# One full 128-column weight load ahead of each set of four 32-column matmuls, in an attention backward pass

## The chip, the cores and the metric

The kernel runs on one core of a Trainium2 chip. The metric is the device time in microseconds (us) of one execution. The kernel before takes 732.7 us (median of 6 runs, 732.21 to 733.62). "Span" is the time from the first to the last instruction of the one execution that was profiled. It is about 1.8 us shorter than the time that was measured of it.

Names: PE is the matrix engine, PEld its weight loads, DVE, ACT and POOL the vector, scalar and general engines, SPq the queue that issues the large transfers. PEclk is the clock granted to PE, as a share of full speed, as the profile shows it.

## The reference, cut to what matters

One token passes a layer of attention over a cache of 8192 positions, with 32 heads of 128, and an MLP beside it. The reference returns the layer's output and the gradients of all inputs and weights.

```python
scores = einsum("bhqd,bhkd->bhqk", q, k) * Dh ** -0.5     # 32 heads, 8192 positions, Dh = 128
p      = softmax(scores)
o      = einsum("bhqk,bhkd->bhqd", p, v)
out    = x + o.reshape(...) @ wo + mlp(xn)
# and by jax.vjp: d_x, d_k_cache, d_v_cache, d_wq, d_wo, d_w1, d_w3, d_w2
```

With a single query, the gradients of K and V are outer products as large as the caches. So 2.10 MB of K and 2.10 MB of V are read for each head, and as many bytes are written: the kernel moves 303.58 MB and does little arithmetic on them.

## The kernel before

K and V of a head lie in tiles of 2.10 MB, of which there are ten. A tile is loaded, turned by PE in 512-column steps, used for the products, **overwritten in place** by its gradient, stored, and only then free for the next load.

```python
def T(h, kind, c):                     # four 128x128 f32 transposes, then one ACT copy
    ...
    for k in range(4):
        nc.tensor.transpose(pT[:, k * P:(k + 1) * P], W3[:, 4 * c + k, :], ident_f[:])
    ...

def Mp(h, kind, c0):                   # "score product": 4 matmuls, one per column tile of 32
    ...
    for c in (c0, c0 + 1):
        ...
        for par in range(2):
            q = QW * (2 * (c - c0) + par)
            o = QL + QW * (2 * a + par) - c0
            nc.tensor.matmul(S_[kind][q:q + QW, :], lhsT=S_["qz"][:, o:o + QW], rhs=KTb[:, par, :],
                             start=(c0 == 0), stop=(c0 == NCH - 2), skip_group_check=True)

def wsum(h, kind, a):                  # "sum product": 16 matmuls, four rounds over the column tiles
    ...
    for i in range(NI):
        q = QW * (i % 4)
        o = QW - 4 + QW * i - 4 * slot
        nc.tensor.matmul(xg["X"][q:q + QW, :], lhsT=Z[:, o:o + QW], rhs=W[:, N4 * i:N4 * (i + 1)], ...)
    ...

def store(kind, h):                    # both in the one queue of SPq, in this order
    ...
    fifo((dkc if kind == "K" else dvc)[h], t[:])
    free_slots.append(t)
    load_next()                        # the next K or V, into the tile that became free longest ago

def outers_a(h):                       # DVE, on the head before
    outer_v(h, 0, J // 2)
    outer_v(h, J // 2, J)
    store("V", h)
    outer_k(h, 0, J // 2)
```

Each head has eight score products and two sum products. The MLP runs once, ahead of head 2.

## Time and profile before

| | kernel before |
|---|---|
| median time, span of the profiled run | 732.7 us, 730.6 us |
| bytes moved, mean rate | 303.58 MB, 416 GB/s |
| rate from 290 to 668 us | 428 GB/s |
| matmuls and weight loads on PE | 5669 and 5669 |
| V gradient of head 2 stored, first transposes of K of head 31, output copy | 122.14, 674.60, 718.11 us |

The prediction shows the slices and the time of a head. What bears on the change besides is the cost of the narrow matmuls and their loads. In the table of groups, "busy, mean ns of one" comes after the first bar; after the second comes the idle time of the engine just before these instructions, and what ended most of it.

```profile
L417 PE MATMUL X<-kv,Z 128*32 128x512 bf16 x1024 | 85.3, 462 | 1.8 <-DVE Z L434 1.8
...
L324 PEld LDWEIGHTS <-qz 128*32 128x32 bf16 x1024 | 26.6, 93 | 42.8 <-issue 41.6
L417 PEld LDWEIGHTS <-Z 128*32 128x32 bf16 x1024 | 28.6, 110 | 33.9 <-issue 16.6
```

1024 sum matmuls take 85.3 us of PE, 83 ns each, although the record gives 462 ns for one: they run side by side. The four of a score product show it best: together they take 0.41 us, and one of them 0.40 us (median of L324). "Issue" is idle time of the load path in which it waited for nothing that the profile shows. Much of it stands ahead of the score products (L324), where PE goes over from 128-wide to 32-wide work.

### The profile page before, as it was taken

Reading aid. Unit: us, or ns where it says so; the run is one execution under the profiler, and the core shown is the slowest. Engines: PE = TensorE matmul, PEld = TensorE weight load, DVE = VectorE, ACT = ScalarE, POOL = GpSimd, SP = SyncE. Lnnn points to the kernel's source line nnn. Section 1 sums busy time; section 2 is a strip of 40 time slices with the busy share of each in tenths; the row PEclk is TensorE's granted clock in tenths of the full one; section 3 lists DMA queues with packets and bytes.
Section 4 is the critical chain, followed back from the end, with each engine's and each line's share of the span. In section 5 each row is a group of like instructions: output and inputs, shape, how many; then the busy total and the mean of one; then the engine's idle time right before and its main releaser. Section 6 shows DMA issues by size and latency. Waiting matters only on the chain.

```text
span 730.6 us, 13869 instructions
## 1 busy us (share of the span) xinstructions
PE 606.6 (83%) x5669; PEld 423.1 (58%) x5669; DVE 459.3 (63%) x806; ACT 369.4 (51%) x719; POOL 29.9 (4%) x45
## 2 busy tenths in 40 slices
PE   3989589998899889988987887888898889978940
PEld 2657466666566656666655555566566556655620
DVE  4069646677757776776646765547756756667482
ACT  2650736656556556554655554545554536655510
POOL 0010110000100000001000000000000000000000
PEclk9996699999999999988998998979897969989765
DMA  9999999999999999999999999999999999999993
GB/s 354 400 411 420 425 421 432 415 429 425 417 416 426 429 427 421 430 428 426 425 428 426 431 423 427 429 428 428 427 424 429 429 427 428 428 434 426 425 393 155
DMA packets 27145, 303.58 MB, mean 416 GB/s; under 512 B 2807, under 2 KB 4153, under 8 KB 10441
## 3 DMA queue, kind: packets, MB, share of 16 engines
q1 hardware_dynamic: 21328, 276.39, 89.5%
q0 software_dynamic: 5728, 26.30, 8.9%
q8 instruction: 44, 0.72, 0.4%
q14 instruction: 21, 0.16, 0.1%
q10 hardware_dynamic: 24, 0.01, 0.0%
HBM read 151.34 MB, written 151.34 MB: 414 GB/s over the span
## 4 chain that ended last, share of the span: by engine, by line
PE 42%; DMA 41%; DVE 8%; ACT 6%; issue 1%; SPq 0%; ACTq 0%; DVEq 0%
DMA out_dram<-kv 22%; PE pT L305 20%; DMA kv<-in_A_k_cache_dram 11%; DMA kv<-in_A_v_cache_dram 7%; PE m L340 6%; PE X L417 5%; ACT KT L307 4%; PE sA L324 4%; DVE kv L450 3%; PE dA L324 2%; DMA wo_g<-in_A_wo_dram 2%; DVE side L251 1%; PE gu_ps L527 1%; ACT KT L330 1%; PE m L430 1%
## 5 line engine op out<-in xcount | busy, mean ns | idle before, releaser
L307 ACT COPY KT<-pT 128x512 f32<-128x512 f32 x512 | 289.5, 589 | 235.3 <-PE pT L305 200.6
L305 PE MATMUL pT<-ident_f,kv 128*128 128x128 f32 x2048 | 318.7, 296 | 40.6 <-DMA kv<-in_A_k_cache_dram 17.9
L305 PEld LDWEIGHTS pT<-ident_f,kv 128*128 128x128 f32 x2048 | 248.5, 154 | 97.0 <-PE pT L305 27.8
L450 DVE TENSOR_TENSOR kv<-qd,U 128x4096 bf16<-128x4096 bf16 x64 | 146.0, 2284 | 0.0
L450 DVE TENSOR_TENSOR kv<-qd,P 128x4096 bf16<-128x4096 bf16 x64 | 143.6, 2284 | 0.0
L340 PEld LDWEIGHTS m<-selc,KT 128*128 128x128 f32 x512 | 67.4, 205 | 45.8 <-ACT KT L330 34.1
L340 PE MATMUL m<-selc,KT 128*128 128x16 f32 x512 | 73.2, 276 | 22.7 <-ACT KT L330 22.5
L417 PE MATMUL X<-kv,Z 128*32 128x512 bf16 x1024 | 85.3, 462 | 1.8 <-DVE Z L434 1.8
L400 DVE SCALAR_TENSOR_TENSOR U<-m,P 128x64 bf16<-128x64 f32 x32 | 7.4, 233 | 104.9 <-PE m L340 104.9
L324 PE MATMUL dA<-KT,qz 128*32 128x512 bf16 x512 | 55.2, 418 | 0.2 <-ACT KT L307 0.2
L324 PE MATMUL sA<-KT,qz 128*32 128x512 bf16 x512 | 55.1, 421 | 0.0
L324 PEld LDWEIGHTS <-qz 128*32 128x32 bf16 x1024 | 26.6, 93 | 42.8 <-issue 41.6
L417 PEld LDWEIGHTS <-Z 128*32 128x32 bf16 x1024 | 28.6, 110 | 33.9 <-issue 16.6
L366 DVE TENSOR_REDUCE mrow<-m 128x1 f32<-128x64 f32 x32 | 7.1, 223 | 62.9 <-PE m L340 62.9
L360 ACT CAST qd<-pT 128x256 bf16<-128x256 f32 x32 | 11.9, 372 | 48.6 <-DVE kv L450 32.4
L500 DVE SCALAR_TENSOR_TENSOR wq_g<-wq_g,side 128x512 bf16<-128x512 bf16 x40 | 27.3, 683 | 0.0
L251 DVE SCALAR_TENSOR_TENSOR side<-wo_g,g_bc 128x640 bf16<-128x640 bf16 x32 | 26.2, 819 | 1.1 <-DMA wo_g<-in_A_wo_dram 0.8
L373 DVE TENSOR_REDUCE negM<-m 128x1 f32<-128x128 f32 x32 | 9.3, 291 | 24.5 <-PE m L370 24.5
L432 DVE SCALAR_TENSOR_TENSOR U<-m,P 128x128 bf16<-128x128 f32 x32 | 11.4, 355 | 18.0 <-PE m L430 18.0
L390 DVE RECIPROCAL rZ<-m 128x1 f32<-128x1 f32 x32 | 5.3, 167 | 24.1 <-PE m L384 24.1
L330 ACT COPY KT<-dA 128x512 f32<-128x512 f32 x32 | 19.3, 604 | 0.6 <-PE dA L324 0.6
L330 ACT COPY KT<-sA 128x512 f32<-128x512 f32 x32 | 19.3, 603 | 0.0
(154 smaller groups left out, 365.2 us busy)
## 6 DMA issues: line engine op xcount, KB each, us to landing
out_dram<-kv SPq DMA_DIRECT2D x64, 2048.0 KB, 31.1
kv<-in_A_k_cache_dram SPq DMA_DIRECT2D x32, 2048.0 KB, 25.2
kv<-in_A_v_cache_dram SPq DMA_DIRECT2D x32, 2048.0 KB, 26.3
out_dram<-wo_g POOLq DMA_DIRECT2D x8, 640.0 KB, 11.4
out_dram<-wq_g POOLq DMA_DIRECT2D x8, 640.0 KB, 12.9
wq_g<-in_A_wq_dram POOLq DMA_DIRECT2D x7, 640.0 KB, 13.2
wo_g<-in_A_wo_dram POOLq DMA_DIRECT2D x7, 640.0 KB, 19.3
kv<-in_B_w_dram SPq DMA_DIRECT2D x2, 1728.0 KB, 28.7
```

The lines of the kernel that those rows point to most:

```text
L251: nc.vector.scalar_tensor_tensor(junk[:], G_["wo"][:, hh, :], 1.0, g_bc[:], ALU.mult, ALU.mult, accum_out=G_["do"][:, hh:hh + 1])
L305: nc.tensor.transpose(pT[:, k * P:(k + 1) * P], W3[:, 4 * c + k, :], ident_f[:])
L307: nc.scalar.copy(KT[:].rearrange("p k w -> p (k w)"), pT[:])
L324: nc.tensor.matmul(S_[kind][q:q + QW, :], lhsT=S_["qz"][:, o:o + QW], rhs=KTb[:, par, :], start=(c0 == 0), stop=(c0 == NCH - 2), skip_grou ...
L330: nc.scalar.copy(XS[:].rearrange("p k w -> p (k w)"), S_.pop(kind)[:])
L340: nc.tensor.matmul(S_["m"][:, b0:b0 + J].rearrange("p (c k t) -> p k c t", k=4, t=2)[:, k, :, :], lhsT=XS[:, k, :], rhs=selc[:].rearrange( ...
L360: nc.scalar.copy(qd[:].rearrange("p a d -> p (a d)"), hd[h].pop("ps_r"))
L373: nc.vector.tensor_reduce(S_["negM"][:], S_["m"][:, 2 * J:2 * J + P], AX.X, ALU.max, negate=True)
L417: nc.tensor.matmul(xg["X"][q:q + QW, :], lhsT=Z[:, o:o + QW], rhs=W[:, N4 * i:N4 * (i + 1)], start=(slot == 0 and i < 4), stop=(slot == NS ...
L432: nc.vector.scalar_tensor_tensor(S_["U2"][:], S_["V"][:, 0:J].unsqueeze(2).to_broadcast([P, J, 2]), S_["m"][:, OC + NS:OC + NS + 1], S_["P ...
L450: nc.vector.tensor_tensor(dst[:, lo * DH:hi * DH].rearrange("p (j a b) -> p j a b", a=DH // 2, b=2), vec.rearrange("p (a b) -> p a b", b=2 ...
L500: nc.vector.scalar_tensor_tensor(wq_g[:, ci, :], wq_g[:, ci, :], 1.0, dqb, ALU.mult, ALU.mult, accum_out=dxa[:, ci, g:g + 1])
```

## The change

Four narrow loads were to become one full one: the four 32-column weights are laid beside each other, one 128-column load is meant to bring in all four, and the four matmuls are marked as holding their weights. The query tile becomes wider for this (and is filled by two small copies), and the vectors of the MLP move into the unused end of a weight tile, to make room.

```diff
-        qz = consts.tile([P, QL + 4 * QW], BF16, name=f"qz{i}")
+        qz = consts.tile([P, QL + 8 * QW], BF16, name=f"qz{i}")
...
+    def held_matmul(out, lhsT, rhs, q, start, stop):
+        E = nc.tensor
+        E.add_instruction(mybir.InstMatmult(
+            ... tile_size=(P, QW), tile_position=(0, q), ..., ldweights=False, ...))
... in Mp
+        o = QL + 2 * QW * 2 * a - c0
+        nc.tensor.ldweights(S_["qz"][:, o:o + P])
-                nc.tensor.matmul(S_[kind][q:q + QW, :], lhsT=S_["qz"][:, o:o + QW], rhs=KTb[:, par, :], ...)
+                held_matmul(S_[kind][q:q + QW, :], S_["qz"][:, o + q:o + q + QW], KTb[:, par, :], q, ...)
... in wsum
-            nc.tensor.matmul(xg["X"][q:q + QW, :], lhsT=Z[:, o:o + QW], rhs=W[:, N4 * i:N4 * (i + 1)], ...)
+            if i % 4 == 0:
+                nc.tensor.ldweights(Z[:, o:o + P])
+            held_matmul(xg["X"][q:q + QW, :], Z[:, o:o + QW], W[:, N4 * i:N4 * (i + 1)], q, ...)
... in mlp, and likewise for eight more vectors
-        sig = consts.tile([P, NB], F32, name="sig")
+        sig = mt(NB)
```

More of the change, by code (lines that the diff above doesn't have):

```diff
@@ L308, in T @@
         hd[h]["kt"][(kind, c)] = KT
+    def held_matmul(out, lhsT, rhs, q, start, stop):
+        E = nc.tensor
+        E.add_instruction(mybir.InstMatmult(
+            name=nc.get_next_instruction_name(), engine=mybir.EngineType.PE,
+            start_tensor_calc=start, stop_tensor_calc=stop, tile_size=(P, QW), tile_position=(0, q),
+            bass_skip_group_check=True, ldweights=False,
+            ins=[E.lower_ap(rhs), E.lower_ap(lhsT, for_matmul_weights=True)], outs=[E.lower_ap(out)]))
     def Mp(h, kind, c0):
@@ L322, in Mp @@
                 q = QW * (2 * (c - c0) + par)
-                o = QL + QW * (2 * a + par) - c0
-                nc.tensor.matmul(S_[kind][q:q + QW, :], lhsT=S_["qz"][:, o:o + QW], rhs=KTb[:, par, :],
-                                 start=(c0 == 0), stop=(c0 == NCH - 2), skip_group_check=True)
+                held_matmul(S_[kind][q:q + QW, :], S_["qz"][:, o + q:o + q + QW], KTb[:, par, :], q,
+                            c0 == 0, c0 == NCH - 2)
     def ev(h, kind):
@@ L346, in fill_qz @@
         g, hh = divmod(h, GH)
-        nc.vector.tensor_copy(
-            hd[h]["qz"][:, QL:QL + 4 * QW].rearrange("p (a t n) -> p a t n", t=2, n=QW)[:, :, :, 0:2],
-            grp[g]["cm"][:, :, :, hh, :].rearrange("p t a m -> p a t m"))
+        for r in range(2):
+            nc.vector.tensor_copy(
+                hd[h]["qz"][:, QL:QL + 8 * QW].rearrange("p (a r t n) -> p r a t n", r=2, t=2, n=QW)[:, r, :, :, 0:2],
+                grp[g]["cm"][:, :, :, hh, :].rearrange("p t a m -> p a t m"))
     def rows_pe(h, ps, first):
@@ L416, in wsum @@
             o = QW - 4 + QW * i - 4 * slot
-            nc.tensor.matmul(xg["X"][q:q + QW, :], lhsT=Z[:, o:o + QW], rhs=W[:, N4 * i:N4 * (i + 1)],
-                             start=(slot == 0 and i < 4), stop=(slot == NS - 1 and i >= NI - 4),
-                             skip_group_check=True)
+            if i % 4 == 0:
+                nc.tensor.ldweights(Z[:, o:o + P])
+            held_matmul(xg["X"][q:q + QW, :], Z[:, o:o + QW], W[:, N4 * i:N4 * (i + 1)], q,
+                        slot == 0 and i < 4, slot == NS - 1 and i >= NI - 4)
         if slot == NS - 1:
@@ L519, with mt @@
     blocks_f = [(b, min(P, F - b * P)) for b in range(NB)]
-    hcol = consts.tile([P, NB], F32, name="hcol")
+    mt_f = mA[:, NA * F:].bitcast(F32)
+    mt_at = [0]
+    def mt(cols):
+        r = mt_f[:, mt_at[0]:mt_at[0] + cols]
+        mt_at[0] += cols
+        return r
+    hcol = mt(NB)
     def mlp():
@@ L546, in mlp @@
                                  start=False, stop=True, skip_group_check=True)
-        gu = consts.tile([P, 2, NB], F32, name="gu")
-        nc.vector.memset(gu[:], 0.0)
+        gu = mt(2 * NB).rearrange("p (w b) -> p w b", w=2)
+        nc.vector.memset(gu, 0.0)
         nc.vector.tensor_copy(gu[:, :, 0:NFULL], gu_ps[:, :, 0:NFULL])
@@ L553, in mlp @@
         up = gu[:, 1, :]
-        dhc = consts.tile([P, NB], F32, name="dhc")
-        nc.vector.tensor_reduce(dhc[:], dh_ps[:], AX.X, ALU.add)
-        sig = consts.tile([P, NB], F32, name="sig")
-        nc.scalar.activation(sig[:], gate, ACTF.Tanh, scale=0.5)
-        nc.vector.tensor_scalar(sig[:], sig[:], 0.5, 0.5, ALU.mult, ALU.add)
-        silu = consts.tile([P, NB], F32, name="silu")
-        nc.vector.tensor_tensor(silu[:], gate, sig[:], ALU.mult)
-        nc.vector.tensor_tensor(hcol[:], silu[:], up, ALU.mult)
@@ L562, in mlp @@
-        hcol_bf = consts.tile([P, NB], BF16, name="hcol_bf")
-        nc.vector.tensor_copy(hcol_bf[:], hcol[:])
-        dgu = consts.tile([P, 2, NB], F32, name="dgu")
-        nc.vector.tensor_tensor(dgu[:, 1, :], dhc[:], silu[:], ALU.mult)
-        t1 = consts.tile([P, NB], F32, name="t1")
-        nc.vector.tensor_scalar(t1[:], sig[:], -1.0, 1.0, ALU.mult, ALU.add)
-        nc.vector.tensor_tensor(t1[:], t1[:], gate, ALU.mult)
-        nc.vector.tensor_scalar(t1[:], t1[:], 1.0, None, ALU.add)
@@ L570, in mlp @@
-        nc.vector.tensor_tensor(t1[:], t1[:], sig[:], ALU.mult)
-        nc.vector.tensor_tensor(dgu[:, 0, :], dhc[:], up, ALU.mult)
-        nc.vector.tensor_tensor(dgu[:, 0, :], dgu[:, 0, :], t1[:], ALU.mult)
-        dgu_bf = consts.tile([P, 2, NB], BF16, name="dgu_bf")
-        nc.vector.tensor_copy(dgu_bf[:], dgu[:])
+        dhc = mt(NB)
+        nc.vector.tensor_reduce(dhc, dh_ps[:], AX.X, ALU.add)
+        sig = mt(NB)
+        nc.scalar.activation(sig, gate, ACTF.Tanh, scale=0.5)
+        nc.vector.tensor_scalar(sig, sig, 0.5, 0.5, ALU.mult, ALU.add)
@@ new lines, in mlp @@
+        silu = mt(NB)
+        nc.vector.tensor_tensor(silu, gate, sig, ALU.mult)
+        nc.vector.tensor_tensor(hcol, silu, up, ALU.mult)
+        hcol_bf = mt(NB // 2).bitcast(BF16)
+        nc.vector.tensor_copy(hcol_bf, hcol)
+        dgu = mt(2 * NB).rearrange("p (w b) -> p w b", w=2)
+        nc.vector.tensor_tensor(dgu[:, 1, :], dhc, silu, ALU.mult)
+        t1 = mt(NB)
+        nc.vector.tensor_scalar(t1, sig, -1.0, 1.0, ALU.mult, ALU.add)
+        nc.vector.tensor_tensor(t1, t1, gate, ALU.mult)
@@ L575, in mlp @@
+        nc.vector.tensor_scalar(t1, t1, 1.0, None, ALU.add)
+        nc.vector.tensor_tensor(t1, t1, sig, ALU.mult)
+        nc.vector.tensor_tensor(dgu[:, 0, :], dhc, up, ALU.mult)
+        nc.vector.tensor_tensor(dgu[:, 0, :], dgu[:, 0, :], t1, ALU.mult)
+        dgu_bf = mt(NB).bitcast(BF16).rearrange("p (w b) -> p w b", w=2)
+        nc.vector.tensor_copy(dgu_bf, dgu)
         for b, rows in blocks_f:
```

## The prediction

> **What bounds the kernel now.** I read the page first, from its slices (part 2): 40 slices of 18.3 us.
>
> ```profile
> PE 606.6 (83%) x5669; PEld 423.1 (58%) x5669; DVE 459.3 (63%) x806; ACT 369.4 (51%) x719; POOL 29.9 (4%) x45
> ...
> DMA  9999999999999999999999999999999999999993
> GB/s 354 400 411 420 425 421 432 415 429 425 417 416 426 429 427 421 430 428 426 425 428 426 431 423 427 429 428 428 427 424 429 429 427 428 428 434 426 425 393 155
> DMA packets 27145, 303.58 MB, mean 416 GB/s; under 512 B 2807, under 2 KB 4153, under 8 KB 10441
> ```
>
> The DMA row is 9 in every slice but the last, at 425 to 430 GB/s. The bytes alone need 303.58 MB / 428 GB/s = 709 us of the 730.6 us span. PE at 83% looks close, so I then asked how long one head takes. The row maximum (L366) runs once per head, and its starts in the timeline give the period. Where no DMA wait stands in the way, four heads go from 162.48 to 235.17 us, 18.2 us a head (the bare head is 17.4 us; each fourth carries group work). From 290.13 to 668.37 us, 18 heads take 21.0 us each. A head moves 4 x 2.10 MB of K and V and their gradients, and a quarter of a group's 4 x 0.655 MB of wq and wo: 9.04 MB, at 428 GB/s 21.1 us. So in the steady part a head waits for bytes, and compute has 21.1 - 18.2 = **2.9 us of slack per head**. The windows view says the same: PE is busy 329 of 378 us, at a granted clock of 0.88[...], against 1.00 in an unhindered head.
>
> ```profile
> core 0: us, PE busy (x) PEld busy (x) DVE busy (x) ACT busy (x) POOL busy (x), PEclk, DMA share, GB/s
> 290.00:668.00 378.00, 328.81 (x2963) 226.81 (x2962) 238.31 (x393) 197.82 (x395) 12.19 (x15) 0.88 1.01 428
> ...
> 233.87:251.24 17.37, 15.52 (x152) 10.81 (x152) 13.63 (x24) 10.40 (x22) 0.00 (x0) 1.00 1.01 427
> ```
>
> Only the **tail** is set by compute: the last heads' work after the last loads landed. In the timeline, K of head 31 (issued at 649.72 us) lets the transposes go at 674.57; the profile names the ACT copy that ended at 674.47, but the PE queue's own semaphore event for a load also stands at 674.5, and such a load takes 25.2 us (median), so I put this wait down to the DMA. From there to the output copy at 718.11 every step is compute, and the last tiny stores end the span at 730.6.
>
> [...] each score product, 32 columns wide, comes after 128-wide transposes with a gap called "issue" of 0.17 us (L324: 41.6 us in all, 223 times), and the next transposes wait about 0.24 us again. [...] 20 full bf16 loads at L488 take 0.74 us together, 37 ns apart, and four 32-column ones at L324 take 0.10 us. So a full load is no cheaper than two narrow ones, and not free. [...]
>
> **The change part by part.** The intent is one full load in place of four narrow ones. The order of the built program says otherwise: the matmuls marked as holding their weights still have **a narrow load each in front of them**. Score and sum products have 2048 matmuls and 2048 narrow loads before and after (L324 and L417 become L312), and 512 full loads are added (L327 and L428, 256 each). Nothing is removed on PE; PE weight loads should go from 5669 to 6181. And each full load[...] stands between 32-wide work.
>
> 1. Score products (8 a head, 4 matmuls each). The full load follows transposes or selection matmuls, also 128-wide[...]. It adds its own time, 0.04 to 0.1 us: 8 x 0.05 = 0.4 us a head.
>
> 2. Sum products (2 a head, 16 matmuls each) are the costly part.
>
> ```profile
> 576.12 0.10 PEld L324 LDWEIGHTS <-qz 128*32 128x32 bf16 x4 [0.17 <-issue]
> 576.12 0.41 PE L324 MATMUL sA<-KT,qz 128*32 128x512 bf16 x4
> ...
> 576.37 0.55 PEld L417 LDWEIGHTS <-Z 128*32 128x32 bf16 x16
> 576.37 1.05 PE L417 MATMUL X<-kv,Z 128*32 128x512 bf16 x16
> ...
> 577.35 0.86 PEld L305 LDWEIGHTS pT<-ident_f,kv 128*128 128x128 f32 x8 [0.42 <-PE X L417]
> ```
>
> Sixteen matmuls pass from 576.37 to 577.35, 0.98 us[...]. The cost of an isolated group of four is read from a score product: its loads begin at 578.37, and the next transposes' loads begin at 578.71, 0.34 us. With a full load of 0.05 to 0.1 us between groups a group becomes about 0.40 us, four 1.6 us[...]: +0.7 us per sum product at full clock. At half clock (granted from about 675 to 686 us) groups are 0.43 us apart now; an isolated score product takes 0.55 us there (645.80 to 646.35), with its load about 0.7: +1.2 us[...].
>
> 3. DVE: 32 more small copies into the query tile, 32 x 0.167 = 5.3 us of 730, in gaps (DVE is 63% busy), off the path. The MLP vectors only change address, into the unused end of a weight tile; the next K or V load into it waits for the gradient store of that weight anyway. Bytes are unchanged.
>
> Sum per head at full clock: 0.4 + 2 x 0.7 = 1.8 us, of which the first sum product partly falls in a PE wait that exists (2 us before L340 at 260.17, for an ACT copy). 18.2 + 1.8 = 20.0 us, still below 21.1. So the steady part **stays with the DMA and costs nothing**. In the tail after 674.57 the path holds the two sum products of head 30 at half clock (2 x 1.2), the first one of head 31 (0.7, the second lies behind 9 us of outer products on DVE), and some 6 score products (6 x 0.05 = 0.3): 3.4 us. 732.3 + 3.4 = 735.7; I say **735.5 us**.
>
> **The rivals.** (a) *All hidden*: the full loads are pulled ahead[...], or delays vanish in the wait for V of head 31. For it: the PE queue runs loads early elsewhere. Against it: [...] V of head 31 leaves at most 2.3 us (its semaphore event at 686.6, its transposes at 688.95). Then 732 to 733. (b) *PE becomes the bound*: if a mode switch costs twice my figure, a head gets 3.6 us more, 21.8 us, over the 21.1 of the DMA, and some 28 heads after the MLP lose 0.7 us each: with the longer tail, 750 us or more. For it: the gap from sum products to transposes is 0.42 us, more than I took for a group's end. Against it: most of that gap is the streaming of the last matmuls, which I counted. The buffer of ten tiles also smooths the heads. (c) *Faster*, as intended: if the chip skipped a narrow load whose weights are there. Nothing in the built program asks for that, and even a free PE could only shorten the tail by some 2 us, since 709 us of bytes and a start at the first loads remain.
>
> **Range and chances.** Low end 731.8: rival (a), with run-to-run noise (732.21 to 732.84). High end 741: the tail at twice its estimate, 7 us, or half clock lasting longer[...], and 1 to 2 us. Leaving the 2% band downward needs 717.7 us, which no PE change reaches here; upward it needs 747, which takes rival (b). I give 0.01 faster, 0.94 same, 0.05 slower.
>
> **What would show each step.** PE weight loads 6181 and 512 full ones: right on the build. Sum products' time from first load to the next transposes near 1.7 us instead of 0.98, with "issue" gaps before L312[...]. DMA row and GB/s unchanged through slice 38, and heads between 290 and 668 us still 21.0 us apart: the slack held. The output copy about 3 us later than 718.11, and the transposes of K of head 31 still near 674.6: the tail. If instead L366 comes every 21.5 us or more and the waits for K and V landings at L305 (17.9 and 12.9 us) are gone, PE has become the bound and I was wrong about the switch; if the sum products still pass in 1.0 us, the full loads hid.

Where "mode" or "switch" stands, read the change between 128 and 32 columns; what the trace of the kernel before shows of it is the gap of 0.17 us at L324. That loads run early is measured: the last four loads of the sum product at 576.37 us are through at 576.93, and its last four matmuls run from 577.03 to 577.42.

Without it a sum product costs 4 x 0.40 - 0.98 = 0.62 us at full clock, where the text has 0.7, and 4 x 0.7 - 4 x 0.43 = 1.08 us at half clock, where it has 1.2. A head then comes to 0.4 + 2 x 0.62 = 1.6 us (the text: 1.8), the tail to 2 x 1.08 + 0.62 + 0.3 = 3.1 us (3.4), and the time to 732.3 + 3.1 = 735.4 us. Compared with the result below are 3.4 and 735.5. All of these costs are estimates from the times beside them.

## The result, and the profile after

The changed kernel takes **736.8 us** (median of 6 runs, 735.79 to 738.06) where the kernel before takes 732.7. The ratio is 1.0058, with a 95% interval from 1.0045 to 1.0071: slower by 4.2 us of 732.7, within the 2% band. Here and below a ratio is the mean time of one kernel's fast runs over that of the other's of the same rounds, so it isn't quite the ratio of the medians. All outputs are right. The run profiled was one of the slower ones, 737.98 us with a span of 736.2 us, 5.6 us over that of before.

From the page of the changed kernel, the counts and the slices of 18.4 us (the line of GB/s reads from left to right; slice 7 is 110 to 129 us):

```profile
PE 639.5 (87%) x5669; PEld 459.9 (62%) x6181; DVE 462.6 (63%) x838; ACT 367.8 (50%) x719; POOL 30.0 (4%) x45
...
DMA  9999998999999999999999999999999999999993
GB/s 347 401 408 422 430 429 355 398 422 412 424 424 425 427 426 427 424 427 428 424 425 426 428 428 420 431 427 428 424 424 427 432 425 432 429 425 433 418 393 143
```

PE weight loads go from 5669 to 6181 and matmuls stay at 5669: nothing was removed, 512 full loads were added. And the transfers have a hole that they did not have before: 355 and 398 GB/s in slices 7 and 8, where the prediction's page of the kernel before has 432 and 415.

The added loads in the table of groups:

```profile
L312 PE MATMUL X<-kv,Z 128*32 128x512 bf16 x1024 | 114.2, 436 | 12.0 <-DVE Z L445 2.0
...
L428 PEld LDWEIGHTS <-Z 128*128 128x128 bf16 x256 | 25.0, 98 | 72.1 <-issue 63.2
...
L327 PEld LDWEIGHTS <-qz 128*128 128x128 bf16 x256 | 28.9, 113 | 0.2 <-issue 0.2
```

Both groups load the same 128 columns, 256 times. Those of the score products (L327) have no idle time ahead of them. Those of the sum products (L428) have 72.1 us, 63.2 of it "issue". The timeline shows one sum product of the changed kernel (start and duration in us first):

```profile
667.23 0.10 PEld L428 LDWEIGHTS <-Z 128*128 128x128 bf16 x1 [0.24 <-DVE Z L445]
667.34 0.10 PEld L312 LDWEIGHTS <-Z 128*32 128x32 bf16 x4
...
667.66 0.10 PEld L428 LDWEIGHTS <-Z 128*128 128x128 bf16 x1 [0.23 <-issue]
667.77 0.10 PEld L312 LDWEIGHTS <-Z 128*32 128x32 bf16 x4
668.10 0.10 PEld L428 LDWEIGHTS <-Z 128*128 128x128 bf16 x1 [0.23 <-issue]
668.21 0.10 PEld L312 LDWEIGHTS <-Z 128*32 128x32 bf16 x4
668.54 0.10 PEld L428 LDWEIGHTS <-Z 128*128 128x128 bf16 x1 [0.23 <-issue]
668.64 0.10 PEld L312 LDWEIGHTS <-Z 128*32 128x32 bf16 x4
668.98 0.75 PEld L305 LDWEIGHTS pT<-ident_f,kv 128*128 128x128 f32 x7 [0.23 <-issue]
```

Ahead of each of its four 128-wide loads, and of the transposes' loads at the end, the load path stands idle for 0.23 to 0.24 us; but for the first, the profile names nothing that was waited for ("issue"). From the first load to the next transposes 1.75 us pass, where the prediction reads 0.98 us in the kernel before: **+0.77 us per sum product, twice a head**. A score product is different:

```profile
672.52 0.10 PEld L327 LDWEIGHTS <-qz 128*128 128x128 bf16 x1
672.72 0.10 PEld L312 LDWEIGHTS <-qz 128*32 128x32 bf16 x4
...
673.06 0.31 PEld L305 LDWEIGHTS pT<-ident_f,kv 128*128 128x128 f32 x3 [0.24 <-PE pT L305]
```

From its narrow loads to the next transposes 0.34 us pass, as in the kernel before:

```profile
578.37 0.10 PEld L324 LDWEIGHTS <-qz 128*32 128x32 bf16 x4 [0.17 <-issue]
...
578.71 0.53 PEld L305 LDWEIGHTS pT<-ident_f,kv 128*128 128x128 f32 x5 [0.24 <-PE pT L305]
```

The full load follows 128-wide transposes without a gap, and the narrow loads start 0.10 us after its end; before, they stood behind a gap of 0.17 us anyway. The added load fits into the gap that was there.

Now where the 5.6 us came in. The first heads, in the windows view (the last three columns are PEclk, the DMA engines' share and GB/s), first of the kernel before, then of the changed one:

```profile
core 0: us, PE busy (x) PEld busy (x) DVE busy (x) ACT busy (x) POOL busy (x), PEclk, DMA share, GB/s
120.00:124.00 4.00, 4.00 (x38) 2.94 (x34) 4.00 (x2) 3.37 (x8) 0.00 (x0) 1.00 1.00 420
124.00:128.00 4.00, 3.70 (x31) 2.72 (x32) 3.14 (x10) 2.89 (x7) 0.00 (x0) 1.00 1.03 440
...
132.00:140.00 8.00, 7.15 (x74) 5.20 (x70) 5.42 (x7) 4.52 (x10) 0.00 (x0) 1.00 1.01 416
```

```profile
120.00:124.00 4.00, 3.86 (x38) 2.77 (x43) 1.95 (x5) 1.17 (x2) 0.00 (x0) 1.00 0.93 392
124.00:128.00 4.00, 3.96 (x37) 2.86 (x41) 4.00 (x3) 2.15 (x4) 0.00 (x0) 1.00 0.21 84
...
132.00:140.00 8.00, 7.33 (x84) 5.17 (x90) 5.08 (x13) 4.47 (x11) 0.00 (x0) 1.00 0.94 360
```

The changed kernel's transfers stop almost wholly for 4 us, at 84 GB/s, because nothing was left to move: the next thing in the queue was a gradient that had not been computed (SPq waits 13.3 us for DVE's product there). The store of V of head 2, from the timeline of SPq, before and after:

```profile
122.14 0.34 SPq L105 DMA_DIRECT2D out_dram<-kv  x1
```

```profile
127.26 0.34 SPq L105 DMA_DIRECT2D out_dram<-kv  x1
```

It comes 5.1 us later. The row maximum, once a head, says where the compute fell behind; the two kernels' lines for heads 2 and 3:

```profile
109.24 0.22 DVE L366 TENSOR_REDUCE mrow<-m 128x1 f32<-128x64 f32 x1 [9.56 <-PE m L340]
124.98 0.22 DVE L366 TENSOR_REDUCE mrow<-m 128x1 f32<-128x64 f32 x1
```

```profile
113.60 0.22 DVE L376 TENSOR_REDUCE mrow<-m 128x1 f32<-128x64 f32 x1 [9.68 <-PE m L349]
130.92 0.22 DVE L376 TENSOR_REDUCE mrow<-m 128x1 f32<-128x64 f32 x1 [0.74 <-PE m L349]
```

Head 3 follows head 2 after 15.7 us before and 17.3 us after: 1.6 us more, two sum products at 0.77. Head 2 itself stands 4.4 us late: 2.1 us had been lost by the row maximum of head 1 (44.91 to 47.03 us; 0.7 of it by that of head 0, which no sum product precedes), and the rest between head 1 and head 2, where the sum products of head 1 and the MLP lie. That stretch varies by some 2 us between executions all the same: it is 62.96 us in e2 and 64.63 in e3 (below), neither with full loads there, and 64.33 before.

An account of bytes puts the loss in its places. The transfers run at some 428 GB/s when they have work. The MB that a stretch of the trace falls short of that rate, from the rates of its 10 us windows, divided by 428 GB/s, is time lost (the end is that of the span):

| MB short of 428 GB/s | 0 to 120 us | 120 to 150 | 150 to 650 | 650 to 680 | 680 to end | all |
|---|---|---|---|---|---|---|
| before | 2.50 | 0.17 | 0.85 | -0.08 | 5.70 | 9.14 |
| after | 2.36 | **1.99** | 1.21 | -0.04 | 5.99 | 11.51 |
| difference, us | -0.3 | **+4.3** | +0.8 | +0.1 | +0.7 | +5.5 |

The hole at 120 to 150 us costs 4.3 of 5.5 us. It is never made good: in no later column is the changed kernel less short than the kernel before. That is why the transposes of K of head 31 start at 680.25 us, not 674.60, and the output copy comes at 723.14, not 718.11. From the one to the other it is 42.9 us after and 43.5 us before. That does not make the full loads free there: from 674 to 686 us the granted clock was 0.57 before and 0.86 after. What they cost at the end is read from e7 below.

### The profile page after: what moved, and what is told of

Read it like the earlier page. It is cut to its first block, busy times and chain, and to the rows that moved or that the text cites. A ratio compares the mean times of both kernels' runs of the same rounds, so it can differ in the third digit from the quotient of the medians.

```text
span 736.2 us, 14414 instructions
## 1 busy us (share of the span) xinstructions
PE 639.5 (87%) x5669; PEld 459.9 (62%) x6181; DVE 462.6 (63%) x838; ACT 367.8 (50%) x719; POOL 30.0 (4%) x45
## 4 chain that ended last, share of the span: by engine, by line
PE 59%; DMA 13%; ACT 9%; DVE 7%; PEld 5%; issue 5%; SPq 0%; ACTq 0%; DVEq 0%
PE pT L305 26%; PE X L312 10%; PE m L349 8%; DMA kv<-in_A_k_cache_dram 7%; PE sA L312 6%; ACT KT L307 6%; DMA out_dram<-kv 5%; PE dA L312 2%; PEld pT L305 2%; DVE kv L461 2%; DVE side L251 2%; DMA wo_g<-in_A_wo_dram 1%; ACT kv L619 1%; ACT KT L339 1%; PE gu_ps L546 1%
## 5 line engine op out<-in xcount | busy, mean ns | idle before, releaser
L305 PE MATMUL pT<-ident_f,kv 128*128 128x128 f32 x2048 | 314.3, 293 | 16.0 <-DMA kv<-in_A_k_cache_dram 12.5
L305 PEld LDWEIGHTS pT<-ident_f,kv 128*128 128x128 f32 x2048 | 244.6, 153 | 64.1 <-PE pT L305 30.3
L312 PE MATMUL X<-kv,Z 128*32 128x512 bf16 x1024 | 114.2, 436 | 12.0 <-DVE Z L445 2.0
L349 PE MATMUL m<-selc,KT 128*128 128x16 f32 x512 | 70.0, 269 | 11.3 <-ACT KT L339 11.3
L349 PEld LDWEIGHTS m<-selc,KT 128*128 128x128 f32 x512 | 63.7, 195 | 25.0 <-ACT KT L339 18.4
L428 PEld LDWEIGHTS <-Z 128*128 128x128 bf16 x256 | 25.0, 98 | 72.1 <-issue 63.2
L327 PEld LDWEIGHTS <-qz 128*128 128x128 bf16 x256 | 28.9, 113 | 0.2 <-issue 0.2
L312 PEld LDWEIGHTS <-Z 128*32 128x32 bf16 x1024 | 26.7, 95 | 3.0
```

Source lines behind the costliest of these rows:

```text
L312: E.add_instruction(mybir.InstMatmult(name=nc.get_next_instruction_name(), engine=mybir.EngineType.PE, start_tensor_calc=start, stop_tenso ...
L327: nc.tensor.ldweights(S_["qz"][:, o:o + P])
L349: nc.tensor.matmul(S_["m"][:, b0:b0 + J].rearrange("p (c k t) -> p k c t", k=4, t=2)[:, k, :, :], lhsT=XS[:, k, :], rhs=selc[:].rearrange( ...
L428: nc.tensor.ldweights(Z[:, o:o + P])
```

## The experiments

Twelve kernels ran, each in five rounds beside the kernel before. "MB short" is the column 120 to 150 us of the account above, from the one profiled run.

| run | what it is | median us | ratio to before, 95% interval | MB short, 120 to 150 |
|---|---|---|---|---|
| e1_first3 | full loads in heads 0 to 2 only | 737.48 | 1.0056 [1.0038, 1.0074] | 1.80 |
| e2_from3 | full loads in heads 3 to 31 only | 735.51 | 1.0033 [1.0018, 1.0048] | 0.12 |
| e3_noload | no full loads, all else of the change | 734.10 | 1.0011 [0.9996, 1.0027] | 0.72 |
| e4_narrow | the added loads made 32 columns wide | 734.21 | 1.0012 [0.9996, 1.0028] | 0.64 |
| e5_sum_only | full loads in sum products only | 736.94 | 1.0048 [1.0036, 1.0061] | 0.75 |
| e6_score_only | full loads in score products only | 733.96 | 1.0007 [0.9995, 1.0020] | 0.20 |
| e7_last2 | full loads in heads 30 and 31 only | 734.15 | 1.0012 [0.9999, 1.0024] | 0.33 |
| e8_mid | full loads in heads 3 to 27 only | 735.14 | 1.0018 [1.0004, 1.0031] | 0.24 |
| e9_after_split2 | the changed kernel, stores of head 2 in halves | 735.85 | 1.0034 [1.0020, 1.0047] | 1.08 |
| e10_tail | kernel before, last head's stores in halves, last group on ACT | 733.80 | 1.0009 [0.9996, 1.0023] | 0.52 |
| e11_early | kernel before, last loads two stores earlier in the queue | 734.53 | 1.0017 [1.0004, 1.0029] | 0.14 |
| e12_all | e10 and e11 together | 735.25 | 1.0026 [1.0010, 1.0042] | 0.49 |

The medians of the kernel before were 733.37 us (beside e1 to e4), 733.61 (e5 to e8) and 733.08 (e9 to e12). That column varies by itself: without full loads in the first heads it is 0.12 to 0.72 MB, so up to 1.4 us of a single profile's time there tell nothing. The column from 680 us to the end varies more: without full loads in the sum products of the last heads it is 5.39 (e1) to 6.57 MB (e8), which is 2.8 us. The main theories at the start were two. *The ramp* (R in the texts): the loss is made in the first heads, where the transfers wait for computed stores. *The tail* (T): it is made after the last loads, as predicted. A third (S) is that it is spread over all heads.

### Which heads: e1 and e2

In both places of the loads, the condition is added:

```diff
-        nc.tensor.ldweights(S_["qz"][:, o:o + P])
+        if h < 3:                      # e1; in e2: if h >= 3
+            nc.tensor.ldweights(S_["qz"][:, o:o + P])
...
-            if i % 4 == 0:
+            if i % 4 == 0 and h < 3:   # e2: and h >= 3
```

> The changed kernel with its full loads in heads 0, 1 and 2 only. Theory R (the ramp: the first heads and the MLP run without DMA slack, the first store of head 2 comes 5 us late and the DMA runs dry between 124 and 136 us): nearly the whole loss stays, about 736 us, DMA under 300 GB/s from 124 to 128 us, the transposes of K of head 31 near 679 instead of 674.6 us. Theory T (the tail, as predicted): the last heads have no full loads, so the time of before, 732.5 us.

> The changed kernel with its full loads in heads 3 to 31 only, 464 of 512. Theory R: no dry DMA at 124 us, transposes of K of head 31 at 674.6 us within 1 us; what is left is the tail, 0 to 3 us by the clock that it happens to get: 732.5 to 735. Theory T: all of the loss, 736 to 737. Theory S (the slack of the middle heads is used up): more than 736, heads between 290 and 668 us more than 21.0 us apart.

Full loads in three heads of 32 cost as much as in all of them: 1.0056 against 1.0058. The windows of 124 to 128 us, of e1 and then of e2:

```profile
124.00:128.00 4.00, 4.00 (x40) 2.88 (x36) 4.00 (x3) 2.56 (x5) 0.00 (x0) 1.00 0.34 142
```

```profile
124.00:128.00 4.00, 3.48 (x40) 2.59 (x42) 3.07 (x11) 2.61 (x6) 0.00 (x0) 1.00 1.06 448
```

The hole is there with the loads of heads 0 to 2 and gone without them. So the ramp alone is enough for most of the loss. But e2 is slower than before too, and theory R missed there: the time is above its 735 us, and the transposes of K of head 31 start at 681.14 us, not near 674.6, without a wait for a transfer. PE was late by itself. The output copy comes at 726.46 us and the span ends only 7.3 us later, where before it is 12.5 us: the tail was late, but the transfers had less left over. Whether the two losses add up can't be told: over e3, which holds all of the change but its full loads (below), e1 loses 0.45% and e2 0.22%, and the full change 0.47%, and the intervals are too wide for the difference. That a slower tail hides behind transfers that are late already is possible, and not shown.

### Loads or switches: e3 and e4

e3 keeps all of the change except the two calls of the full load (`if False:`). e4 keeps the count of 6181 loads, but makes the added ones narrow, so that the width does not change between the groups:

```diff
-                nc.tensor.ldweights(Z[:, o:o + P])
+                nc.tensor.ldweights(Z[:, o:o + QW], tile_position=(0, 0))
```

> The changed kernel without the 512 full loads: what is left is the wider query tile with its second small copy, and the MLP vectors at another address. All theories: as before, 732.5 us within 0.7; if the two small parts cost something it shows here as 1 us or more.

> The 512 added loads stay in their places but are 32 columns wide at column 0[...]. If the mode switch[...] is the cost: a sum product takes 1.0 to 1.1 us again from first load to next transposes instead of 1.75, and the time is 732.5 to 733.5. If the loads themselves, or their place in the queue, are the cost: about 736 us, as with the full loads.

One sum product of e4 in the timeline, an added narrow load ahead of each four:

```profile
621.49 0.09 PEld L428 LDWEIGHTS <-Z 128*32 128x32 bf16 x1
621.49 0.12 PEld L312 LDWEIGHTS <-Z 128*32 128x32 bf16 x7
621.50 1.05 PE L312 MATMUL X<-kv,Z 128*32 128x512 bf16 x16
...
621.96 0.10 PEld L312 LDWEIGHTS <-Z 128*32 128x32 bf16 x1
622.47 0.86 PEld L305 LDWEIGHTS pT<-ident_f,kv 128*128 128x128 f32 x8 [0.41 <-PE X L312]
```

It takes 0.98 us again, with as many loads as in the changed kernel, and the 256 added ones at L428 have 4.7 us of idle time ahead of them, where they had 72.1. So it isn't the added instructions that cost, it is the **change of width** between 128 and 32 columns. Both kernels come out at 0.1% over before, which their intervals don't tell from nothing; in us they missed the times expected, by 0.9 and 0.7, but the kernel before ran 0.7 us longer beside them too, 733.37 us against 732.7 at the start. e10 shows the same 0.1%, though it leaves the first 680 us alone, so this is where these comparisons stop resolving.

### Which products: e5 and e6

> The changed kernel with only the 256 full loads of the sum products. In the trace of the changed kernel a score product begins its narrow loads 0.16 us after the transposes' loads end, as before with 0.17: its full load fits in that gap; a sum product takes 1.75 us instead of 0.98. So all of the loss should be here: 736 to 737.5 us. The prediction's own split (0.4 us a head from score products, 1.4 from sum products) would put about a fifth of it in the other run.

> The changed kernel with only the 256 full loads of the score products. If they hide in the gap after the transposes: the time of the run without any full load, 733.5 to 734.3 us. If they cost 0.05 us or more each on the path: 0.4 us a head, some 1 us more at the ramp and the tail.

e5 drops the full load of the score products, e6 that of the sum products (`if False:` and `and False` in the lines shown). The sum products carry the cost, 1.0048, and the score products none that can be seen, 1.0007. The heads agree: from the row maximum of head 5 to that of head 9, e6 takes 72.67 us and the kernel before 72.69.

e5's profile has a misfit: its hole in the ramp is small (0.75 MB, as in e3 without any full load), and most of its loss lies after 680 us (6.75 MB short, 5.70 before). Its output copy comes at 727.27 us. The trace shows a part of the reason. From head 0 to head 1 e5 was granted a clock of 1.00 and took 18.99 us, the changed kernel 0.92 and 20.28 us (each with the same wait of 1.47 us in head 0), and the stretch to head 2 took 64.07 us instead of 66.57; so its store of V of head 2 went at 124.16 us, not 127.26. From head 2 to head 3 it takes 17.30 us, as the changed kernel does. So the size of the hole depends on the clock and on that stretch too, and two executions of nearly the same work can lose their time at different ends. Why e5 is late at its end stays open.

### The later heads apart: e7 and e8

The condition is `h >= 30` in e7 and `3 <= h < 28` in e8.

> Full loads in heads 30 and 31 only. Theory T (the tail, with 3.4 us): 735.5 to 737, and the output copy 2 to 4 us after 718.1 us at equal clock. Theory that the loss is in the ramp alone: as without full loads, 734 us. The run with full loads from head 3 on lost 2 us, so I expect 735 to 736.

> Full loads in heads 3 to 27 only, 400 of 512. If the middle heads have slack (21.1 us of bytes against some 19.6 us of work) they cost nothing: 733.5 to 734.5 us, and K of head 31 lands within 1 us of the run without full loads. If the loss of the run from head 3 on came from the middle: 735.5 us.

Neither stands out against e3: 1.0012 and 1.0018 against 1.0011. I had expected 735 to 736 us of e7; it takes 734.15. The predicted cost of the tail, 3.4 us or 0.46%, is not in e7: its interval ends at 0.24%. Its trace shows what became of the three sum products that were counted there. The two of head 30 stand ahead of a wait for V of head 31, which is 1.45 us in e7, 1.55 in e3 and 1.50 in e8, so their delay is covered. From the end of that wait to the output copy it is 31.58 us in e7, and 30.48 in both e3 and e8, which have no full loads in these heads: **+1.1 us**, 0.9 of it at the first sum product of head 31.

Together with heads 28 and 29 e7 and e8 are e2, which is at 0.33%, and their intervals are too wide to say where in heads 3 to 31 that comes from. This stays open. One thing is seen in e2: after a wait of 3.32 us for K of head 30 PE runs at half clock for 15 us, busy all the while.

```profile
657.50:672.50 15.00, 14.65 (x81) 9.54 (x92) 7.24 (x7) 4.08 (x7) 0.00 (x0) 0.50 1.01 422
```

e9, with a wait of 3.27 us at the same place, does the same. In the changed kernel the waits for K of heads 30 and 31 are 1.69 and 1.22 us, and the windows give about 3.4 us of half clock after each. In the kernel before it is about 10 us, after a wait of 2.67 us ahead of the transposes of K of head 31. In e2 and e9, and in e5, PE comes to K of head 31 without a wait, and the transfers fall short a second time: from 700 to 710 us they move 272, 343 and 284 GB/s, where e3 has 405 (e2 is at 125 from 700 to 705). In these profiles the tail is set by compute, as predicted, by a lateness that was brought along from earlier heads.

### Filling the hole: e9

If the transfers starve for the stores of head 2, smaller stores that can go earlier should fill the hole. In the changed kernel, for head 2 alone:

```diff
     def outers_a(h):
         outer_v(h, 0, J // 2)
+        if h in SPLIT:                       # SPLIT = (2,), HALF = KVN // 2
+            store_lo("V", h)                 # the first half, 1 MB, at once
         outer_v(h, J // 2, J)
         store("V", h)                        # stores the rest; likewise for K
```

> The changed kernel, with the V and K gradient stores of head 2 issued in two halves of 1 MB, the first as soon as its half of the outer products is done. Theory R (the loss is made in the first three heads, where the transfers wait for the computed stores of head 2): the first half of V is issued about 2 us before 127.3 us, the dip of the changed kernel (84 GB/s from 124 to 128 us, 360 from 132 to 140) is filled for the most part, the MB moved at 140 us are 56.5 or more (55.6 in the changed kernel, 57.3 in the kernel before), and the ratio falls from 1.0058 to 1.001 to 1.003 (734 to 735.5 us). Rival (the loss is made in the tail or spread over all heads): the same 737, ratio 1.005 to 1.006.

The windows of e9 over the same time as above:

```profile
124.00:128.00 4.00, 4.00 (x40) 3.03 (x39) 4.00 (x3) 2.72 (x6) 0.00 (x0) 1.00 0.90 369
...
132.00:140.00 8.00, 7.33 (x82) 5.35 (x88) 4.57 (x15) 3.96 (x11) 0.00 (x0) 1.00 1.00 358
```

The first half of V goes at 124.29 us, 3.0 us before the whole one did, and the rate from 124 to 128 us is 369 instead of 84 GB/s. From 132 to 140 us it stays as low as in the changed kernel, 358 and 360. The shortage falls from 1.99 to 1.08 MB, by 2.1 us of transfers, and the ratio from 1.0058 to 1.0034, by 1.8 us of 732.7 (the two intervals just meet, so this size is rough). Loss and shortage shrink together, with no change to PE's program. It is less than I had expected (1.001 to 1.003, and 56.5 MB or more moved at 140 us, where it is 56.4): the stores of head 2 remain late as a whole, since the compute in front of them does. The same split without full loads was not run, so a gain of its own isn't excluded; with 0.17 MB short before, there is little for it to win.

### Trying to beat both: e10, e11 and e12

e10 halves the stores of head 31 in the same way and gives the last group's scaling of wo and wq to ACT. e11 puts the loads of K and V of head 31 two stores earlier in the queue, by asking for one free tile instead of three:

```diff
+        if len(pending) == 2:
+            lag[0] = 1
+            load_next()
+            load_next()
```

> The kernel before, with the gradient stores of head 31 issued in halves and the last group's wo and wq scaling on ACT instead of DVE: an attempt to beat both kernels in the tail. If the last stores set the end (12.5 us from the output copy to the end of the span), the end comes 1 to 3 us sooner: 730.5 to 732.5, ratio 0.996 to 0.999. If the end is set by what the transfers still owe when the last head is done, nothing: 1.000.

> The kernel before, with the loads of K and V of head 31 issued two stores earlier in the queue. If the tail starts with the landing of K of head 31 (transposes at 674.6 us in the kernel before), these start some 3 to 5 us earlier and the time falls by 1 to 3 us: ratio 0.996 to 0.999. If the bytes owed in front of it and behind it set the end, the head starts earlier and the end stays: 1.000.

> The edits of the two attempts before together (stores of head 31 in halves, last group's scaling on ACT, K and V of head 31 loaded earlier), on the kernel before. If compute after the last load sets the end: 727 to 731 us, ratio 0.993 to 0.998. If the bytes set it (303.58 MB at 428 GB/s after the ramp), 731 to 733, ratio 0.998 to 1.000.

All three are slower or the same. e11 is the telling one: its output copy comes at 713.75 us, 4.4 us sooner than before, and yet its span is 732.7 us, 2.1 us longer.

```profile
650.00:660.00 10.00, 8.96 (x66) 5.95 (x67) 5.37 (x13) 5.08 (x11) 0.00 (x0) 0.69 0.85 349
660.00:670.00 10.00, 10.00 (x97) 7.33 (x97) 8.48 (x11) 5.96 (x11) 0.00 (x0) 1.00 0.89 297
```

The two loads are issued no sooner: at 650.46 and 660.46 us, and at 649.72 and 659.65 before. A load that stands earlier in the queue waits there until its tile's old gradient is written out (SPq waits 71.0 us for such stores from 620 to 715 us, 50.9 us before), and finished stores wait behind it. The transfers fall to 297 GB/s and are 2.11 MB short from 650 to 680 us; they have that much more to move at the end. So the output copy doesn't set the end: the bytes do, wherever in the run they were held up. No kernel that I tried beats the kernel before. An eleventh tile, which would give the transfers more to do in the ramp, was not run.

## Why the prediction was right or wrong

The class was right, and so was the range: 735.5 us predicted with 731.8 to 741.0, 736.8 us measured. The reason was wrong in its main point, so the number was luck.

- **Nothing removed, 512 loads added**: right, 6181 loads.
- **Sum products +0.7 us each at full clock**: right, 0.77 measured, and e4 shows that it is the change of width (0.98 us without it, 1.75 with it). At half clock a score and a sum product together take 3.21 us (584.88 to 588.09) where they took 2.26 us before (681.84 to 684.10): +0.95 where 1.2 was predicted. The gaps ahead of the full loads are 0.44 us there.
- **Score products +0.4 us a head**: wrong, 0. The step that failed is "It adds its own time": the load is hidden in the gap of 0.17 us that the trace had shown ahead of the score products (e6: 1.0007, and 72.67 us for four heads against 72.69). A reading behind it was off too: 37 ns for a full load, read at half clock (0.50 from 705 to 710 us), is less than two narrow ones at 25 ns each, where the prediction has it no cheaper.
- **20.0 us per head, below 21.1**: right in effect; the 20.0 itself was not measured. With no wait for DMA, four heads take 78.3 us (168.63 to 246.91), 19.6 each. But e3, without full loads, takes 78.5 us there (164.05 to 242.53), at a granted clock of 0.89; it was 0.93 in the changed kernel, 0.98 in the one before. Where both have full clock, a head takes 19.32 us (209.37 to 228.69) against 18.46 in e3 (205.11 to 223.57): +0.9, not 1.5. A part falls in PE's wait for an ACT copy, as predicted: in these four heads it is 5.7 us before and 2.2 after. From 290 to 668 us the rate is 426 GB/s after and 428 before: the slack held. It shrank, though: the transposes' waits for K and V fell from 17.9 + 12.9 us to 12.5 + 0.8. The sign that I had named for it, heads 21.0 us apart, was a bad one. From head 12 to head 30 they are 20.4 us apart (308.73 to 675.17), because compute stood 18.6 us behind the kernel before at head 12 and, with tiles loaded ahead of it, caught up to 6.8 us.
- **"Only the tail is set by compute"**: this step failed. The ramp is set by compute as well. I had read the heads' period from 162 us on and the slices, which are 9 from the start, and took that for slack everywhere. "425 to 430 GB/s" in every slice but the last was a misreading: the first four have 354, 400, 411 and 420. Slack of 2.9 us a head exists where a head waits for bytes; from head 1 to head 3 the bytes wait for a head. There two sum products a head add 1.5 us, and the store of V of head 2 went out 5.1 us late. The hole cost 4.3 us of 5.5 in the profiled run. e1, e2 and e9 show it: it comes with the loads of three heads, goes without them, and the loss shrinks as it is filled. e5 shows its limit: with the same sum products its hole was hardly larger than e3's, and the time was lost all the same.
- **Tail +3.4 us**: too large; +1.1 us on the way to the output copy (e7 against e3 and e8), and nothing in e7's time that can be told from e3. The two sum products of head 30 (2 x 1.2) vanish in the wait for V of head 31, as rival (a) had it. In the changed kernel K's transposes came 5.6 us later instead of "near 674.6". What e2 loses without the ramp is 0.2% over e3, and its place is open. The half clock that I expected to make the tail dearer lasted about 3.4 us after K of head 31 landed, against about 10 us before; it is not a fixed part of the tail.
- **DVE copies and MLP vectors free**: not contradicted. e3 holds them alone, at 1.0011, from -0.04% to 0.27%.

So 3.2 us were predicted for a place that lost 0.7, and most of the 4.2 us measured came from a place that I had counted as free. The number was right because two errors met.

## What to carry to other kernels

A mean rate near the best that the transfers show (here 416 GB/s over the span, 428 from 290 to 668 us) does not mean slack on every head: look for the first stores that transfers depend on, and ask what a slower compute does there, since the transfers may not win it back: here they lost 4.3 us from 120 to 150 us, ran on at 426 GB/s (290 to 668 us), and made up none of it. Before replacing narrow weight loads by a wide one, look at what stands on both sides: between narrow matmuls each full load cost a wait of 0.23 us here, behind wide work it cost nothing that could be seen (e6: 1.0007). And count the loads of the built program, since a matmul marked as holding its weights may still get one: here all 2048 narrow loads stayed, and 5669 loads became 6181.
